# Gate and up both as seven products of half sums, their blocks interleaved

## The chip, the core and the metric

The kernel runs on one core of a Trainium2 chip. A core has five engines with a queue each: TensorE (PE in the profile; PEld is its weight loads), VectorE (DVE), ScalarE (ACT), GpSimd (POOL), and SyncE (SP), which only issues DMAs here. SBUF holds the operands; TensorE writes its products to PSUM, eight banks of 512 f32 columns for each of 128 partitions. The metric is device time in microseconds of one execution; lower is better.

## What is computed

A layer norm of x (2048 tokens x 512), a linear-attention branch A, a gated branch B, and their sum with x. The change lies in B's first two matrix products, gate and up:

```python
def _B_ref(x, w_gate, w_up, w_down):          # x: 2048 x 512
    g = jnp.einsum("bsd,df->bsf", x, w_gate)  # w_gate: 512 x 1792
    u = jnp.einsum("bsd,df->bsf", x, w_up)    # w_up:   512 x 1792
    h = g * u
    return jnp.einsum("bsf,fd->bsd", h, w_down)

x = A_x
xn = _layernorm(x, axis=-1)
return x + _A_ref(xn, A_wqkv, A_w_phi, A_wo) + _B_ref(xn, B_w_gate, B_w_up, B_w_down)
```

Branch A makes features from Q and K (exponentials of a projection, of both signs, each normalised), sums K's features times V over all tokens, and reads that sum out with Q's features.

## The kernel before

**Tiling.** The 512 model columns are four slices of 128 (contracted over), the 1792 gate and up columns are 14 slices `ft`, and tokens are 16 tiles of 128, or four groups `sg` of 512. The normalised tokens lie transposed in `xnT`. A product "weights slice x 512 tokens" is a group of four matmuls of 512 columns into one PSUM bank. `U(ft, sg)` makes gate and up in this plain way: the gate bank goes through a ScalarE copy (`ge`) to a bf16 slot, and VectorE multiplies the up bank by it (`h`) into `hT`.

**Seven products.** For token groups 1 and 2 and the pairs `(ft, ft+7)` with `ft` below `NB = 6`, `up` is made as a 2 x 2 block product (rows: `ft` and `ft+7`; columns: the two token groups; contraction split into two halves) with seven half products in place of eight (`BLOCK`, L821). A half product is two matmuls of 512 columns. It needs sums of token blocks, X1 to X4 (`XSUMS`, L781: eight VectorE steps, once), and sums of weight blocks, S1 to S4 (`WSUMS`, L792: four GpSimd steps of 256 columns for each block, two slots in `Su_v`). The steps of a block: P1 goes to bank `pa` and is copied by ScalarE to a second bank `c` (the seed); P2 is added on `c`; P6, P5 and P3 are added to `pa` one after the other, with what stands there read out in between (a snapshot by ScalarE, an add by VectorE); P7 and P4 go to bank `pb`. Gate is made plainly beside it (`G`, L800): four groups of four matmuls per block, spread between the block's products (L1072 to L1078).

**Down.** The product with `w_down` is of the same seven-product kind (`DOWN_STEPS`, pairs of token tiles), with sums T of `w_down` and S of `h` on GpSimd (L737 too, 512 and 896 columns wide). Its VectorE steps (L961) add the residual x.

**Banks.** In the block stage banks 0 and 1 are `pa` and `pb`, banks 6 and 7 gather K times V, and banks 2 to 5 are a ring from which `nb()` (L624) hands out one after the other: to gate products, K features, V, the seed bank.

**Order of work.** The program adds steps in one order (the loop at L1111: for each token tile K, V, then as many `units` as `PACE` asks). `_plan` (L199) then plays this list forward with a cost for each step and writes a fixed order for every queue: of the steps ready within a window of 60 ns it takes the one with the lowest `prio`, then the lowest place in the program. On the chip each queue runs in that order; a step waits on semaphores for what it needs. The costs: a matmul `n / 2.4 + 2.5` ns (L459), a VectorE step `60 + 1.045 n` (L452), a ScalarE step `50 + 0.835 n` (L444); `prio` is 0 everywhere.

**Lines in the profile.** L482 all matmuls; L437 ScalarE copies, exponentials and the seeds; L737 the sums (X on VectorE, the others on GpSimd); L679 reduces of K and Q features; L685 and L687 their even-up on GpSimd; L712 V's eviction on VectorE; L813 the gated product of a block; L819 its adds; L765 the gated product of `U`; L961 the down stage's adds.

Of the kernel before, what the change touches and what calls it, by code (L numbers as in the profile page):

```python
# [21 lines left out]
NQ = D // 128  # L22
# [327 lines left out]
NB = 6  # L350
NSW = 2
# [9 lines left out]
def _build(nc, es, A_x, A_wqkv, A_w_phi, A_wo, B_w_gate, B_w_up, B_w_down, out):  # L361
# [102 lines left out]
    def seed(o, src, name):  # L464
        act_op(o, src, name=name)
        seeded[(o.offset % 4096) // 512] = True
# [55 lines left out]
    def load_x(eng, t0, n, after=None):  # L522
        o = sbv("x", t0 * 512, n * 512)
        return sc.dma(eng, o.rearrange("p (t d) -> p t d", t=n),
               x_flat[t0 * 128:(t0 + n) * 128, :].rearrange("(t p) d -> p t d", p=128), n * 131072,
               writes=[o], name=f"x{t0}", after=after)
# [97 lines left out]
    def nb():  # L624
        b = ring_banks[0][rp[0] % len(ring_banks[0])]
        rp[0] += 1
        return b
# [44 lines left out]
    def features(Et, w, t, sm, name):  # L672
        b = nb()
        mm(group(bank(b), [(xnT(q, t * 128, 128), Wp_v[:, w, q, :]) for q in range(NQ)]), name=f"{name}{t}")
        ev = Et.rearrange("p (h s f) -> p h s f", h=H, s=2)
        src = bank(b).rearrange("p (h f) -> p h f", h=H)
        act_op(ev[:, :, 0, :], src, func=ACTF.Exp, name=f"{name}e{t}")
        act_op(ev[:, :, 1, :], src, func=ACTF.Exp, scale=-1.0, name=f"{name}e{t}")
        dve(lambda e: e.tensor_reduce(out=sm, in_=Et.rearrange("p (h f) -> p h f", f=16), axis=AX.X, op=ALU.add),  # L679
            [Et], [sm], cost=1130.0, name=f"{name}r{t}")  # L680
        return ev
# [87 lines left out]
    Su_v = sbv("tf", 0, NSW * 1024).bitcast(F16).rearrange("p (r w k j) -> p r w k j", r=NSW, w=4, k=2)  # L769
    sn_v = sbv("oring", 0, 3 * 512).bitcast(F16).rearrange("p (r s) -> p r s", r=3)  # L770
    snc = [0]
    gw = {}

    def snap():
        snc[0] += 1
        return sn_v[:, snc[0] % 3, :]
# [15 lines left out]
    def WSUMS(ft):  # L792
        S1, S2, S3, S4 = (Su_v[:, ft % NSW, w] for w in range(4))
        A = lambda i, k: wA(wu_v, i, k, ft)
        sums(POOL, S3, A(0, 0), A(1, 0), ALU.subtract, f"w3.{ft}")
        sums(POOL, S1, A(1, 0), A(1, 1), ALU.add, f"w1.{ft}")
        sums(POOL, S2, S1, A(0, 0), ALU.subtract, f"w2.{ft}")
        sums(POOL, S4, A(0, 1), S2, ALU.subtract, f"w4.{ft}")

    def G(ft, sg):  # L800
        i = gctr[0] % 6
        gctr[0] += 1
        g = sbv("gring", i * 512, 512) if i < 4 else sbv("tf", 2048 + (i - 4) * 512, 512)
        gw[ft, sg] = g
        b = nb()
        mm(group(bank(b), [(wg_v[:, q, ft * 128:(ft + 1) * 128], xnT(q, sg * 512, 512)) for q in range(NQ)]),
           name=f"g{ft}.{sg}")
        act_op(g, bank(b), name=f"ge{ft}.{sg}")

    def gated(ft, sg, src):  # L810
        h = hT_v[:, ft, hs(sg * 512):hs(sg * 512) + 512]
        g = gw[ft, sg]
        dve(lambda e: e.tensor_tensor(out=h, in0=src, in1=g, op=ALU.mult), [src, g], [h], name=f"h{ft}.{sg}")  # L813
# [4 lines left out]
    def add(o, src, sn, name):  # L818
        dve(lambda e: e.tensor_tensor(out=o, in0=src, in1=sn, op=ALU.add), [src, sn], [o], name=name)  # L819

    def BLOCK(ft, banks):  # L821
        ft2 = ft + NF // 2
        A = lambda i, k: wA(wu_v, i, k, ft)
        S1, S2, S3, S4 = (Su_v[:, ft % NSW, w] for w in range(4))
        X1, X2, X3, X4 = (Tx_v[:, w] for w in range(4))
        pa, pb = bank(banks[0]), bank(banks[1])
        st = {}

        def p1():
            xprod(pa, A(0, 0), xB(0, 1), True, f"b1.{ft}")  # L830
            st["c"] = bank(nb())
            seed(st["c"], pa, f"sd.{ft}")

        def p7():
            xprod(pb, S3, X3, True, f"b7.{ft}")
            st["p7"] = snap()
            act_op(st["p7"], pb, name=f"s7.{ft}")

        def p2():
            xprod(st["c"], A(0, 1), xB(1, 1), False, f"b2.{ft}")  # L840
            gated(ft, 1, st["c"])

        def p6():
            xprod(pa, S2, X2, False, f"b6.{ft}")
            st["u2"] = snap()
            act_op(st["u2"], pa, name=f"s2.{ft}")

        def p4():
            xprod(pb, A(1, 1), X4, False, f"b4.{ft}")
            add(pb, pb, st["u2"], f"a4.{ft}")  # L850
            gated(ft2, 1, pb)

        def p5():
            xprod(pa, S1, X1, False, f"b5.{ft}")
            add(pb, pa, st["p7"], f"a5.{ft}")
            gated(ft2, 2, pb)

        def p3():
            xprod(pa, S4, xB(1, 2), False, f"b3.{ft}")
            gated(ft, 2, pa)  # L860
# [208 lines left out]
    blocks = [BLOCK(ft, (0, 1)) for ft in range(NB)]  # L1069
    gs = [(G, f, sg) for ft in range(NB) for sg in (1, 2) for f in (ft, ft + NF // 2)]  # L1070
    units += [(XSUMS, XENG), (WSUMS, 0), (WSUMS, 1)] + gs[:4]
    for ft in range(NB):  # L1072
        p1, p7, p6, p2, p4, p5, p3 = blocks[ft]
        g4 = gs[4 * ft + 4:4 * ft + 8]
        seqs = [(p1,), (p7,)] + g4[:1] + [(p6,), (p2,)] + g4[1:2] + [(p4,)] + g4[2:3] + [(p5,)] + g4[3:] + [(p3,)]
        if ft + NSW < NB:
            seqs.append((WSUMS, ft + NSW))
        units += seqs  # L1078
# [53 lines left out]
    assert ui[0] >= NA  # L1132
    down = DOWN_STEPS(0)
# [91 lines left out]
```

## Time and profile before

| what | before |
|---|---|
| median of 4 runs | 217.71 us (215.18 to 218.83) |
| the profiled execution | 217.41 us, its span 215.4 us |
| granted TensorE clock | 1.000 |
| TensorE matmul busy | 208.1 us, 1609 recorded |
| VectorE, ScalarE, GpSimd busy | 153.6, 113.2, 138.1 us |
| HBM read, written | 8.67 MB, 2.10 MB |

The span runs from the first to the last instruction; the time of an execution has some 2 us more around it. Matmuls are pipelined: the duration of one, 379 ns for 512 columns, is its latency, and the next starts before it ends. A row of a group reads: line, engine, operation, output and inputs with their shapes, count, then busy us, mean ns of one, and the idle time before such instructions with what ended it.

### The profile page before, as it was taken

What the parts mean: (1) busy time and instruction counts of PE and PEld (TensorE: products, weight loads), DVE (VectorE), ACT (ScalarE), POOL (GpSimd) and SP (SyncE); (2) the same over time, 40 slices, a digit from 0 to 9 for tenths busy, and PEclk for the clock granted to TensorE, in tenths of its full rate; (3) what the DMA queues carried; (4) which work ended last, traced back from release to release, by engine and by line L of the source; (5) the groups of instructions that cost most, each with busy time, mean ns of one, the idle gap of its engine ahead of it and who ended that gap; (6) DMA issues with size and microseconds to landing.
All of it is one profiled execution on the core that took longest, in us unless ns stands there. A gap on an engine that the chain in (4) does not pass through costs nothing.

```text
span 215.4 us, 4228 instructions
## 1 busy us (share of the span) xinstructions
PE 208.1 (97%) x1619; PEld 138.6 (64%) x1642; DVE 153.6 (71%) x301; ACT 113.2 (53%) x286; POOL 138.1 (64%) x167
## 2 busy tenths in 40 slices
PE   8999999959999999999999999999999999999995
PEld 2775444425445444444546788898888888888984
DVE  4857599774948687695987884786666776568663
ACT  4656999769885759787732432334333243342000
POOL 4070644249999999995490289784977779422540
PEclk9999999999999999999999999999999999999999
DMA  5999799891100000222020145154173433514421
GB/s 171 325 258 358 208 138 87 249 264 24 27 0 0 3 0 0 49 50 52 0 49 3 36 80 131 24 77 97 27 124 71 99 75 71 127 30 96 96 77 52
DMA packets 48660, 19.96 MB, mean 93 GB/s; under 512 B 37376, under 2 KB 48640, under 8 KB 48640
## 3 DMA queue, kind: packets, MB, share of 16 engines
q1 hardware_dynamic: 47968, 19.36, 39.5%
q10 hardware_dynamic: 672, 0.33, 0.6%
q8 instruction: 13, 0.21, 0.4%
q14 instruction: 7, 0.06, 0.1%
HBM read 8.67 MB, written 2.10 MB: 50 GB/s over the span
## 4 chain that ended last, share of the span: by engine, by line
PE 82%; ACT 5%; DVE 5%; DMA 4%; issue 1%; POOL 1%; SPq 1%; DVEq 0%
PE ps L482 82%; ACT arena L437 5%; DMA arena<-in_B_w_up_dram 2%; DVE arena L679 2%; DVE arena L737 2%; DMA arena<-arena 1%; SPq L173 1%; DVE arena L712 1%; POOL arena L687 0%; POOL arena L605 0%; DVE arena L765 0%; POOL arena L685 0%; DVE arena L871 0%; DVE arena L961 0%; ACT arena L715 0%
## 5 line engine op out<-in xcount | busy, mean ns | idle before, releaser
L482 PE MATMUL ps<-arena 128*128 128x256 bf16 (+5 forms) x1609 | 203.8, 287 | 4.1 <-DVE arena L712 2.4
L482 PEld LDWEIGHTS ps<-arena 128*128 128x128 bf16 (+1 forms) x1632 | 137.3, 98 | 71.1 <-DVE arena L712 3.0
L437 ACT ACTIVATE arena<-ps 128x512 bf16<-128x512 f32 (+3 forms) x167 | 83.1, 534 | 72.6 <-PE ps L482 68.8
L737 POOL TENSOR_TENSOR arena<-arena 128x896 f16<-128x896 f16 (+3 forms) x72 | 91.9, 1288 | 24.3 <-PE ps L482 18.8
L679 DVE TENSOR_REDUCE arena<-arena 128x64 f32<-128x1024 bf16 x32 | 38.8, 1215 | 14.1 <-ACT arena L437 14.1
L437 ACT ACTIVATE arena<-arena 128x32 f32<-128x32 f32 (+4 forms) x96 | 28.9, 313 | 12.6 <-DVE arena L679 9.7
L687 POOL TENSOR_TENSOR arena<-arena 128x512 bf16<-128x512 bf16 x32 | 33.8, 1057 | 1.2
L961 DVE TENSOR_TENSOR arena<-ps,arena 128x256 f32<-128x256 f32 (+1 forms) x56 | 23.5, 421 | 11.7 <-PE ps L482 11.5
L685 POOL TENSOR_TENSOR arena<-arena 128x32 f32<-128x32 f32 x32 | 8.5, 266 | 24.6 <-ACT arena L437 24.6
L813 DVE TENSOR_TENSOR arena<-ps,arena 128x512 f16<-128x512 f32 x24 | 16.3, 687 | 7.5 <-PE ps L482 7.2
L871 DVE TENSOR_TENSOR arena<-ps,arena 128x256 f16<-128x256 f32 x32 | 13.4, 420 | 10.6 <-ACT arena L437 10.6
L712 DVE TENSOR_TENSOR arena<-ps,arena 128x512 bf16<-128x512 f32 x16 | 10.9, 683 | 2.0 <-PE ps L482 1.4
L765 DVE TENSOR_TENSOR arena<-ps,arena 128x512 f16<-128x512 f32 x14 | 9.6, 684 | 3.7 <-PE ps L482 2.3
L596 DVE BATCH_NORM_STATS2 arena<-arena 128x6 f32<-128x512 bf16 x16 | 10.5, 675 | 2.3 <-DMA arena<-in_A_x_dram 2.1
L919 DVE TENSOR_TENSOR arena<-ps,arena 128x512 bf16<-128x512 f32 x16 | 11.0, 690 | 0.4
L819 DVE TENSOR_TENSOR ps<-ps,arena 128x512 f32<-128x512 f32 x12 | 8.3, 694 | 3.4 <-PE ps L482 3.2
L605 POOL TENSOR_SCALAR arena<-arena 128x1 f32<-128x1 f32 x12 | 3.0, 265 | 9.6 <-ACT arena L437 9.6
L578 POOL TENSOR_TENSOR arena<-arena 128x128 bf16<-128x128 bf16 x4 | 1.6, 426 | 8.7 <-DMA arena<-in_A_w_phi_dram 8.7
L915 DVE RECIPROCAL arena<-arena 128x32 f32<-128x32 f32 x16 | 5.6, 350 | 0.4
L1038 PE MATMUL ps<-const-bfloat16-1.0 128*128 128x512 bf16 x10 | 4.4, 626 | 0.8 <-PEq L1210 0.8
L737 DVE TENSOR_TENSOR arena<-arena 128x512 f16<-128x512 bf16 x8 | 3.9, 531 | 1.1 <-DMA arena<-arena 1.1
L715 ACT ACTIVATE arena<-arena 128x32 bf16<-128x32 f32 x16 | 3.7, 231 | 0.3
(20 smaller groups left out, 24.0 us busy)
## 6 DMA issues: line engine op xcount, KB each, us to landing
arena<-in_B_w_down_dram SPq DMA_DIRECT2D x1, 1792.0 KB, 7.9
out_dram<-arena SPq DMA_DIRECT2D x14, 128.0 KB, 2.0
arena<-in_A_x_dram SPq DMA_DIRECT2D x3, 512.0 KB, 8.9
arena<-in_B_w_gate_dram SPq DMA_DIRECT2D x1, 768.0 KB, 7.4
arena<-in_B_w_up_dram SPq DMA_DIRECT2D x1, 768.0 KB, 7.9
arena<-arena SPq DMA_TRANSPOSE x44, 3.0
arena<-in_B_w_gate_dram SPq DMA_DIRECT2D x2, 256.0 KB, 4.7
arena<-in_B_w_gate_dram SPq DMA_DIRECT2D x1, 512.0 KB, 6.2
```

Source lines behind the costliest of these rows:

```text
L437: return e.activation(out=out_ap, in_=in_ap, func=func, scale=scale, **kw)
L482: ins = e.matmul(o, lhsT=l, rhs=r, start=s, stop=p, skip_group_check=True)
L596: dve(lambda e, t=t: e.bn_stats(stats_v[:, t, :], x_tile(t)), [x_tile(t)], [stats_v[:, t, :]], cost=560.0, name=f"st{t}", win=win)
L679: dve(lambda e: e.tensor_reduce(out=sm, in_=Et.rearrange("p (h f) -> p h f", f=16), axis=AX.X, op=ALU.add), [Et], [sm], cost=1130.0, name= ...
L687: pool(lambda e: e.tensor_tensor(out=ev[:, :, 1, :], in0=ev[:, :, 1, :], in1=ratio[:, :, None].to_broadcast([128, H, 16]), op=ALU.mult), [ ...
L712: dve(lambda e: e.tensor_tensor(out=o1, in0=src, in1=rp_[:, :, :, None].to_broadcast([128, 8, 4, 16]), op=ALU.mult), [src, rs_v[:, t % 4, ...
L737: fn = lambda e: e.tensor_tensor(out=out_, in0=a_, in1=b_, op=op)
L765: dve(lambda e: e.tensor_tensor(out=h, in0=bank(bu), in1=g, op=ALU.mult), [bank(bu), g], [h], name=f"h{ft}.{sg}")
L813: dve(lambda e: e.tensor_tensor(out=h, in0=src, in1=g, op=ALU.mult), [src, g], [h], name=f"h{ft}.{sg}")
L871: dve(lambda e: e.tensor_tensor(out=h, in0=bank(b, 256, 256), in1=g, op=ALU.mult), [bank(b, 256, 256), g], [h], name=f"h{ft}.{s_lo}")
L919: dve(lambda e: e.tensor_tensor(out=ov, in0=src, in1=wv4[:, :, :, None].to_broadcast([128, 8, 4, 16]), op=ALU.mult), [src, w], [o], cost=6 ...
L961: dve(lambda e: e.tensor_tensor(out=out_, in0=in_ps, in1=in_sb, op=ALU.add), [in_ps, in_sb], [out_], cost=328.0, name=f"{name}.{p}")
```

## The change

Gate is also made of seven half products for the six pairs. `BLOCK` takes a kind, `"u"` or `"g"`: gate blocks use bank 1 as `pa`, up blocks bank 0. `pb` is no fixed bank any more: P7 takes one from the ring and holds it until after P4, and the seed bank is held from P1 until after P2; `nb()` passes over held banks. P5's sum of an up block takes another ring bank. Where an up block ends in gated products, a gate block writes its results to gate slots: two by ScalarE copies, two straight from VectorE's adds.

A gate block stands one block ahead of its up block, and the products of up block `ft` and gate block `ft+1` are interleaved. GpSimd makes weight sums for both kinds. The gate sums, gate snapshots and a seventh gate slot lie in the space of x tiles 4 to 11, which have been normalised by then; two DMAs load these tiles again before the down stage. Seeds, snapshots and gate copies get priority -1 on ScalarE, adds and gated products -1 on VectorE. The reduce of the features can be cut into `RS` parts; `RS` is 1, so it is as before.

```diff
+RS = 1
+PA = -1
+PD = -1
@@
-    def nb():
-        b = ring_banks[0][rp[0] % len(ring_banks[0])]
-        rp[0] += 1
+    held = set()
+
+    def nb(hold=False):
+        assert not held.issuperset(ring_banks[0])
+        while True:
+            b = ring_banks[0][rp[0] % len(ring_banks[0])]
+            rp[0] += 1
+            if b not in held:
+                break
+        if hold:
+            held.add(b)
         return b
@@
-    Su_v = sbv("tf", 0, NSW * 1024).bitcast(F16).rearrange("p (r w k j) -> p r w k j", r=NSW, w=4, k=2)
-    sn_v = sbv("oring", 0, 3 * 512).bitcast(F16).rearrange("p (r s) -> p r s", r=3)
-    snc = [0]
+    xz = layout["x"] + 4 * 512
+    S_w = {"u": sbv("tf", 0, NSW * 1024), "g": arena[:, xz:xz + NSW * 1024]}
...
+    sn_v = {"u": sbv("oring", 0, 3 * 512), "g": arena[:, xz + 2048:xz + 2048 + 3 * 512]}
...
+    gslots = ([sbv("gring", i * 512, 512) for i in range(4)] + [sbv("tf", 2048 + i * 512, 512) for i in range(2)]
+              + [arena[:, xz + 3584:xz + 4096]])
@@
-    def BLOCK(ft, banks):
+    def BLOCK(kind, ft, ba):
...
         def p1():
-            xprod(pa, A(0, 0), xB(0, 1), True, f"b1.{ft}")
-            st["c"] = bank(nb())
-            seed(st["c"], pa, f"sd.{ft}")
+            xprod(pa, A(0, 0), xB(0, 1), True, "b1" + nm)
+            st["ci"] = nb(True)
+            st["c"] = bank(st["ci"])
+            seed(st["c"], pa, "sd" + nm)
 
         def p7():
-            xprod(pb, S3, X3, True, f"b7.{ft}")
-            st["p7"] = snap()
-            act_op(st["p7"], pb, name=f"s7.{ft}")
+            st["bi"] = nb(True)
+            st["b"] = bank(st["bi"])
+            xprod(st["b"], S3, X3, True, "b7" + nm)
+            st["p7"] = snap(kind)
+            act_op(st["p7"], st["b"], name="s7" + nm, prio=PA)
...
         def p4():
-            xprod(pb, A(1, 1), X4, False, f"b4.{ft}")
-            add(pb, pb, st["u2"], f"a4.{ft}")
-            gated(ft2, 1, pb)
+            pb = st["b"]
+            xprod(pb, A(1, 1), X4, False, "b4" + nm)
+            if kind == "u":
+                add(pb, pb, st["u2"], "a4" + nm)
+                gated(ft2, 1, pb)
+            else:
+                add(gslot(ft2, 1), pb, st["u2"], "a4" + nm)
+            held.discard(st["bi"])
 
         def p5():
-            xprod(pa, S1, X1, False, f"b5.{ft}")
-            add(pb, pa, st["p7"], f"a5.{ft}")
-            gated(ft2, 2, pb)
+            xprod(pa, S1, X1, False, "b5" + nm)
+            if kind == "u":
+                pt = bank(nb())
+                add(pt, pa, st["p7"], "a5" + nm)
+                gated(ft2, 2, pt)
+            else:
+                add(gslot(ft2, 2), pa, st["p7"], "a5" + nm)
@@
-    units += [(XSUMS, XENG), (WSUMS, 0), (WSUMS, 1)] + gs[:4]
+    gb = [BLOCK("g", ft, 1) for ft in range(NB)]
+    ub = [BLOCK("u", ft, 0) for ft in range(NB)]
+    units += [(XSUMS, XENG), (WSUMS, "g", 0), (WSUMS, "u", 0), (WSUMS, "g", 1), (WSUMS, "u", 1)]
+    p1, p7, p6, p2, p4, p5, p3 = gb[0]
+    units += [(f,) for f in (p1, p7, p2, p6, p4, p5, p3)]
     for ft in range(NB):
...
         if ft + NSW < NB:
-            seqs.append((WSUMS, ft + NSW))
-        units += seqs
+            units.append((WSUMS, "g", ft + NSW))
+        u = ub[ft]
+        g = gb[ft + 1] if ft + 1 < NB else [None] * 7
+        p1, p7, p6, p2, p4, p5, p3 = u
+        q1, q7, q6, q2, q4, q5, q3 = g
+        units += [(f,) for f in (p1, p7, p2, p6, q1, q7, p4, q2, p5, q6, p3, q4, q5, q3) if f is not None]
+        if ft + NSW < NB:
+            units.append((WSUMS, "u", ft + NSW))
@@
     assert ui[0] >= NA
+    load_x(SP, 4, 4, name="rx")
+    load_x(SP, 8, 4, name="rx")
```

## The prediction, made before the changed kernel was run

> **What bounds the kernel now.** I read the page's forty slices first, then a table by stretches of time, then the timeline around the one hole, then the groups by shape for prices. The slices (each digit is the busy share of 5.4 us, in tenths):
>
> ```profile
> PE   8999999959999999999999999999999999999995
> DVE  4857599774948687695987884786666776568663
> ACT  4656999769885759787732432334333243342000
> POOL 4070644249999999995490289784977779422540
> ```
>
> TensorE is full from start to end except for one slice, the ninth (43 to 48 us). GpSimd is full through the ten slices after it. The table by stretches gives busy us of each engine; the block stage (the 512-token products of gate and up for tokens 512 to 1535) runs from about 41 to 116 us:
>
> ```profile
> 41.00:47.00 6.00, 3.62 (x23) 1.62 (x22) 6.00 (x12) 3.97 (x12) 2.11 (x4) 1.00 1.13 323
> 47.00:58.00 11.00, 10.92 (x69) 5.54 (x71) 6.46 (x10) 9.85 (x23) 11.00 (x14) 1.00 0.20 48
> 82.00:94.00 12.00, 11.95 (x70) 5.69 (x70) 8.65 (x12) 9.73 (x26) 12.00 (x17) 1.00 0.12 23
> 105.00:116.00 11.00, 10.89 (x75) 5.78 (x76) 9.43 (x14) 4.98 (x14) 6.26 (x6) 1.00 0.13 24
> ```
>
> Columns: stretch, TensorE, weight loads, VectorE, ScalarE, GpSimd, then clock, DMA share, GB/s. Before 47 us VectorE is busy without a break and TensorE waits; from 47 us TensorE is busy without a break at the full clock (1.00), beside ScalarE at 9.85 of 11 early and VectorE at 9.43 of 11 late. The hole in TensorE's timeline, and VectorE's work in it:
>
> ```profile
> 39.72 4.95 PE L482 MATMUL ps<-arena 128*128 128x512 bf16 x28
> 47.02 3.19 PE L482 MATMUL ps<-arena 128*128 128x512 bf16 x14 [2.36 <-DVE arena L712]
> ```
> ```profile
> 39.21 0.43 DVE L737 TENSOR_TENSOR arena<-arena 128x512 f16<-128x512 bf16 x1 [1.09 <-DMA arena<-arena]
> ...
> 41.88 2.35 DVE L737 TENSOR_TENSOR arena<-arena 128x512 f16<-128x512 bf16 x4
> 44.16 1.21 DVE L679 TENSOR_REDUCE arena<-arena 128x64 f32<-128x1024 bf16 x1
> 45.29 1.08 DVE L737 TENSOR_TENSOR arena<-arena 128x512 f16<-128x512 bf16 x3
> 46.29 0.68 DVE L712 TENSOR_TENSOR arena<-ps,arena 128x512 bf16<-128x512 f32 x1
> ```
>
> The token sums X (L737 on VectorE, eight of them) stand ahead of the V eviction (L712), and that eviction holds the PSUM bank that the next gate product needs. Prices by shape (busy us, mean ns):
>
> ```profile
> L482 PE MATMUL ps<-arena 128*128 128x512 bf16 x413 | 98.3, 379 | 3.6 <-DVE arena L712 2.4
> L437 ACT ACTIVATE arena<-ps 128x512 bf16<-128x512 f32 x110 | 60.4, 597 | 31.6 <-PE ps L482 28.6 <-DVE arena L813 2.6
> L737 POOL TENSOR_TENSOR arena<-arena 128x256 f16<-128x256 bf16 x22 | 14.5, 667 | 0.6 <-DMA arena<-in_B_w_up_dram 0.4
> L482 PE MATMUL ps<-arena 128*128 128x512 f16 x48 | 14.1, 379 | 0.0
> L437 ACT ACTIVATE arena<-ps 128x512 f16<-128x512 f32 x12 | 7.1, 594 | 0.8 <-PE ps L482 0.8
> L819 DVE TENSOR_TENSOR ps<-ps,arena 128x512 f32<-128x512 f32 x12 | 8.3, 694 | 3.4 <-PE ps L482 3.2
> ```
>
> The 379 ns is latency. The price of a 512-column matmul is its spacing: 14 of them take 3.19 us, so (3.19 - 0.379) / 13 = 0.216 us; f16 operands show the same 379.
>
> **TensorE.** Per block, four gate products of four matmuls (16) become seven of two (14). Six blocks: 12 matmuls fewer, 12 x 0.216 = 2.6 us, all on the path, since TensorE is what ends every stretch from 47 us on. A rule speaks against counting this: the Trainium skill, "Perfetto Trace Analysis", section Identifying the Most-Contended Engine, says that matmul busy time is no measure of headroom and weight-load busy time (or FLOPs against peak) is. Weight loads fill 5.54 of 11 us here, half; taken by that figure TensorE would have room and the 12 matmuls would be worth 0. The spacing of 0.216 us for 512 columns leaves no room between matmuls (one load of 98 ns hides behind each), so I take 2.6.
>
> **Start of the stage.** X still waits for the transposes that land at 39.2 us and still takes until 46.4. Before, TensorE had three plain gate products (2.6 us), which need no X, ahead of the hole. After, the first gate block can run P1 and P2 without X; P7 needs X3 (there at 43.9), P6 needs X2 (45.7), P4 needs X4 (46.4). Five products of 0.43 = 2.16 us get done by the time V's bank comes free at 47.0, against 2.6 before: the hole costs 0.4 more. Bounds: 2.4 us gained if the queue's order fills it, 2 us lost if P7 and what stands behind it on TensorE (a KV product, K of tile 5) come late and push their own followers.
>
> **GpSimd.** Four more weight sums per block, 24 x 0.667 = 16.0 us. The first two gate sets (5.3 us) read weights and scratch that are free once tiles 4 to 7 are normalised (about 27 us), and GpSimd idles some 6 us between there and 39 us, so they lie beside other work. The other 10.7 us fall into the saturated stretch, and what yields is the W_down sums (L737, 512 wide: 12 x 1.154) and the first pairs' S sums, which now run early as filling. GpSimd idles 3.3, 0.8, 0.9, 5.3 and 4.5 us at gaps between 99 and 124 us, 14.8 in all, which takes 10.7: cost 0, up to 2 us if W_down sums or the first S3 come after P7 of the down stage wants them (it starts at 117). A second rule: the Trainium skill, "SBUF — State Buffer", section Who interferes with whom, says a VectorE instruction with two SBUF inputs blocks against a GpSimd one that reads SBUF. The trace has it: four X sums took 2.35 us while K's even-up multiply (L687, 42.50 for 1.12 us) ran on GpSimd, where three took 1.08. By the rule at its worst each of the eight X sums could wait out one gate weight sum, 8 x 0.667 = 5.3 us more hole. I take 0, since the first sets fit in before 39 us, and the new VectorE adds have one input in PSUM.
>
> **VectorE.** Two more adds per block, 12 x 0.69 = 8.3 us, one block earlier than the gated products that use them. VectorE goes from about 8.7 to 10 of 12 us in the middle stretch: covered, but at 85%. **ScalarE.** 24 gate evictions (14.3 us) become 30 seeds, snapshots and evictions (6 x 5 x 0.597 = 17.9): 3.6 more, covered, tight in 47 to 58, where it has 1.15 us free.
>
> **Queue order and banks.** The order of each queue is frozen by the planner, which counts 595 ns for a 512-wide VectorE step and 478 for a ScalarE one; the rows say 690 and 597. So every hand-over is some 0.1 us late where TensorE has nothing in reserve. Today the four plain gate products per block are that reserve; after, both kinds are chains of hand-overs. Three to four tight hand-overs in each of five double blocks at 0 to 0.1: 0 to 2 us, I take 0.8, near the low end because the page shows only 4.1 us of waits for all 1609 matmuls. The priorities for chain steps cost nothing of themselves; what they delay is K's and Q's exponentials and reduces and V's evictions, which hold ring banks. Bounds -0.5 to +5, taken as 0 here; it is the slow rival.
>
> **Reload of x.** Two DMAs of 512 KB on SP, 0.5 us of issue each. They wait for the last gate blocks' reads (near 100 to 110 us); behind them stand the fourth Q transpose (107) and the first output transposes (120). Tile 4's x is first read in the down stage's third pair, near 144 us; x loads took 8.9 us to land in the crowded start and the DMA share here is 0.1 to 0.3. Cost 0; if the wait held SP to 120, the 1 MB would cost at most 1 to 2 us.
>
> **Sum.** -2.6 + 0.4 + 0.8 = -1.4 us on the profiled execution, whose time is 217.4 (span 215.4 and 2.0 around it): 216.0. The median of the runs is 0.3 higher: 216.3.
>
> **Rivals.** (1) Likeliest, 216.3, own range 214.8 to 219: 0.42. (2) The hole closes: products of up's first block, which need only tokens and a free bank, are drawn forward into it. Then 2.6 + 2.4 to 2.85 are saved: 212.5. For it: P1 and P2 of both kinds need no X. Against: VectorE is busy for all six us of that stretch, and everything else waits for it. 0.20. (3) Slower: the ring runs out of banks. The ring has four banks in this stage (2 to 5). In a double block up's P7 bank, gate's P2 bank and gate's P7 bank are all held between gate's P7 and up's P4, leaving one for K and V, whose evictions (two exponentials of 0.6, or 0.68 on VectorE) now stand behind the chain steps. If two such products per double block wait one eviction and one chain step, 0.6 + 0.6, half of them with a 0.43 filler ahead, TensorE loses about 1.8 us per double block, 9 in five: 217.7 - 2.2 + 9 = 224.5. It decides beyond a 2% loss from 1.3 us per double block (6.6 in all). For it: the only hole today is just this, a bank held by a late eviction, and ScalarE, VectorE and GpSimd stand at 80 to 100%. Against: from 47 us on nothing of the kind shows. 0.33. (4) The change doesn't shorten the end: late W_down or S sums on GpSimd give the 2.2 us back at 114 to 120: 217.7 to 218.5. 0.05.
>
> **Numbers.** Faster by over 2% (below 213.4) is rival 2 alone: 0.20. Slower by over 2% (above 222.1) is rival 3: 0.33. Within 2%, about what a measurement of this kernel can tell from no change: 0.47. The predicted time is the likeliest, 216.3. Both signs together hold more than it does, so the 8-in-10 range runs from the middle of rival 2 to just past rival 3's value, 212.5 to 225.0.
>
> **What would show it.** Right: TensorE has 12 fewer 512-wide matmuls, its hole before the first blocks lasts 2.5 to 3.5 us, waits after 47 us stay under 2 us, and the down stage's first product starts near 114.5 us instead of 116.1. Rival 2: no hole over 1 us. Rival 3: repeated TensorE waits of 0.5 to 2 us between 50 and 110 us, released by ScalarE exponentials or VectorE L712. Rival 4: a wait on GpSimd L737 at 113 to 120 us. A longer hole at 41 to 47 beside weight sums on GpSimd would make my reading of the port rule wrong; a stall of x reads near 144 us that of the reload.

## The result, and the profile after

| | before | after |
|---|---|---|
| median of the runs | 216.65 us (64 runs) | 215.35 us (43 runs) |
| range | 215.14 to 218.83 | 214.53 to 217.20 |
| profiled execution, its span | 217.41, 215.4 us | 214.46, 212.5 us |

The ratio is 0.9963, with an interval of 0.9947 to 0.9978: faster, by less than 2%. The kernel before, at 217.71 over its first four runs, stands at 216.65 over 64.

The times after are not one cluster. Of 44 executions 27 have a granted clock of 0.999 or more (median 214.99) and 17 have 0.991 or 0.992 (median 216.68). Of 80 executions of the kernel before beside the experiments below, one had less than the full clock. The profiled execution after is one at the full clock. The page's forty slices after:

```profile
PE   8899999699999999999999999999999999999995
DVE  4847599996969698999977866686666876568653
ACT  4656989679986889888722533424433243332000
POOL 4070697439999999999999695875958779422640
PEclk9999999999999999999999999999999999999999
```

TensorE's one thin slice is still there, one place earlier (37 to 43 us). GpSimd is now full over thirteen slices in a row, where it was over nine. The table by stretches of the kernel after (stretch, length, TensorE, weight loads, VectorE, ScalarE, GpSimd, clock, DMA share, GB/s):

```profile
41.00:47.00 6.00, 4.38 (x27) 2.12 (x29) 5.93 (x11) 4.49 (x12) 2.33 (x5) 1.00 0.99 274
47.00:58.00 11.00, 10.95 (x77) 5.58 (x77) 9.04 (x14) 10.71 (x28) 11.00 (x17) 1.00 0.07 15
82.00:94.00 12.00, 11.95 (x69) 5.61 (x69) 11.12 (x16) 10.62 (x29) 12.00 (x18) 1.00 0.23 44
105.00:116.00 11.00, 10.76 (x77) 5.84 (x78) 8.46 (x15) 2.61 (x6) 11.00 (x8) 1.00 0.33 84
```

ScalarE rose from 9.85 to 10.71 of 11 us in the second row and VectorE from 8.65 to 11.12 of 12 in the third, and TensorE beside them has as little idle time as before. The last row has lost a little: 10.76 instead of 10.89, with GpSimd full. Line numbers have moved: L485 are the matmuls, L440 ScalarE's copies, exponentials and seeds, L753 the sums, L838 the adds of a block, L694 K's and Q's reduces, L701 and L703 their even-up, L728 V's eviction, L781 the gated product of `U`. The groups by shape (busy us, mean ns, idle before them):

```profile
L485 PE MATMUL ps<-arena 128*128 128x512 bf16 x353 | 85.1, 379 | 1.2
L485 PE MATMUL ps<-arena 128*128 128x512 f16 x96 | 26.3, 379 | 2.0 <-DVE arena L753 2.0
L753 POOL TENSOR_TENSOR arena<-arena 128x256 f16<-128x256 bf16 x40 | 26.4, 676 | 1.5 <-PE ps L485 1.0 <-DMA arena<-in_B_w_up_dram 0.3
L838 DVE TENSOR_TENSOR ps<-ps,arena 128x512 f32<-128x512 f32 x12 | 8.3, 692 | 2.1 <-PE ps L485 1.5 <-ACT arena L440 0.7
L838 DVE TENSOR_TENSOR arena<-ps,arena 128x512 bf16<-128x512 f32 x12 | 8.0, 682 | 0.0
L440 ACT ACTIVATE ps<-ps 128x512 f32<-128x512 f32 x12 | 7.1, 594 | 2.3 <-PE ps L485 2.0
```

The 512-column matmuls are 449 instead of 461: 12 fewer (f16 ones have doubled, bf16 ones gone down by 60). VectorE's adds and ScalarE's seeds have doubled. The 2.0 us before the f16 matmuls is the hole, and what ends it is now an X sum (L753). TensorE's timeline around it (start, busy, and idle before it with what ended it):

```profile
36.74 3.87 PE L485 MATMUL ps<-arena 128*128 128x512 bf16 x24
42.57 5.18 PE L485 MATMUL ps<-arena 128*128 128x512 f16 x29 [1.95 <-DVE arena L753]
```

and VectorE's timeline in the same stretch:

```profile
37.76 1.29 DVE L753 TENSOR_TENSOR arena<-arena 128x512 f16<-128x512 bf16 x3 [0.51 <-DMA arena<-arena]
38.98 1.20 DVE L694 TENSOR_REDUCE arena<-arena 128x64 f32<-128x1024 bf16 x1
40.10 0.67 DVE L781 TENSOR_TENSOR arena<-ps,arena 128x512 f16<-128x512 f32 x1
40.70 0.67 DVE L728 TENSOR_TENSOR arena<-ps,arena 128x512 bf16<-128x512 f32 x1
41.30 2.22 DVE L753 TENSOR_TENSOR arena<-arena 128x512 f16<-128x512 bf16 x4
```

The first group of matmuls ends with V's product of tile 3. Next in TensorE's queue is P7 of the first gate block, ahead of P1 and P2, and it needs X3. X3 comes in the last line, behind K's reduce (L694), a gated product of U (L781) and a V eviction (L728), 2.5 us of VectorE work, none of which needs X. The first of its four sums is the second half of X3. It took 1.21 us, and each of the other three 0.41; GpSimd's even-up of K ran beside it:

```profile
41.30 1.21 DVE L753 TENSOR_TENSOR arena<-arena 128x512 f16<-128x512 bf16 x1
```
```profile
41.17 1.06 POOL L703 TENSOR_TENSOR arena<-arena 128x512 bf16<-128x512 bf16 x1
```

So 0.8 us of the hole is this meeting. All five traces with this order have it (1.21 to 1.23 us for that sum), and the kernel before had the like (1.27 us for the same sum, in the 2.35 us of the prediction's row).

**Where the time went.** A single span says little to within 1 us: over the traces of this study V's product of tile 3, ahead of the hole, starts anywhere between 39.6 and 41.2 us. So TensorE's time was cut at fixed matmuls, start to start, and each part split into work (512 columns at 0.216 us, others by the planner's n / 2.4 + 2.5 ns; matmuls without a record are counted from the kernel's own order) and the rest, called lost:

| us | before | after |
|---|---|---|
| hole (V's product of tile 3 to that of tile 4), lost | 2.54 | 2.13 |
| from there to the last K times V product, lost | 0.14 | 0.52 |
| from there to the last matmul, lost | 0.12 | 0.13 |
| all three: work | 170.00 | 167.41 |
| all three: lost | 2.80 | 2.79 |

Work is down by 2.59 us; what is lost is the same. It lies mostly in two places: the hole, and one wait near 109 us that costs TensorE 0.3. The wait in TensorE's table of waits, as its weight loads show it (sum, count, longest) and, below it, GpSimd's timeline there:

```profile
PEld ps L485 <- POOL arena L703: 0.6, 1, 0.6
```
```profile
104.60 1.89 POOL L753 TENSOR_TENSOR arena<-arena 128x896 f16<-128x896 f16 x1
...
106.66 1.89 POOL L753 TENSOR_TENSOR arena<-arena 128x896 f16<-128x896 f16 x1
108.49 1.06 POOL L703 TENSOR_TENSOR arena<-arena 128x512 bf16<-128x512 bf16 x1
```

The even-up of the last K (L703) stands behind sums of 1.89 us on a GpSimd that has no pause; the last K times V product needs it and stands at the head of TensorE's queue.

### The profile page after: what moved, and what is told of

It is laid out like the page before. It is cut to its first block, busy times and chain, and to the rows that moved or that the text cites. A ratio compares the mean times of both kernels' runs of the same rounds, so it can differ in the third digit from the quotient of the medians.

```text
span 212.5 us, 4265 instructions
## 1 busy us (share of the span) xinstructions
PE 205.1 (97%) x1607; PEld 136.8 (64%) x1630; DVE 160.0 (75%) x313; ACT 115.5 (54%) x292; POOL 152.7 (72%) x191
## 3 DMA queue, kind: packets, MB, share of 16 engines
q1 hardware_dynamic: 49024, 20.41, 40.8%
## 4 chain that ended last, share of the span: by engine, by line
PE 71%; POOL 17%; issue 3%; DMA 2%; DVE 2%; ACT 2%; SPq 1%; DVEq 0%
PE ps L485 71%; POOL arena L753 12%; POOL arena L703 3%; DMA arena<-in_B_w_up_dram 2%; ACT arena L440 1%; POOL arena L701 1%; SPq L173 1%; DVE arena L753 1%; DVE arena L694 1%; DVE arena L728 0%; DVE arena L781 0%; ACT ps L440 0%; DVE arena L910 0%; DVE arena L1000 0%; DVEq L343 0%
## 5 line engine op out<-in xcount | busy, mean ns | idle before, releaser
L485 PE MATMUL ps<-arena 128*128 128x256 bf16 (+5 forms) x1597 | 201.2, 286 | 4.1 <-DVE arena L753 2.0
L485 PEld LDWEIGHTS ps<-arena 128*128 128x128 bf16 (+1 forms) x1620 | 135.6, 98 | 70.1 <-DVE arena L753 2.4
L753 POOL TENSOR_TENSOR arena<-arena 128x256 f16<-128x256 bf16 (+3 forms) x96 | 107.7, 1139 | 21.9 <-PE ps L485 16.4
L440 ACT ACTIVATE arena<-ps 128x512 bf16<-128x512 f32 (+3 forms) x167 | 82.9, 537 | 67.4 <-PE ps L485 63.4
L694 DVE TENSOR_REDUCE arena<-arena 128x64 f32<-128x1024 bf16 x32 | 38.9, 1215 | 11.2 <-ACT arena L440 11.2
L440 ACT ACTIVATE arena<-arena 128x64 f32<-128x64 f32 (+4 forms) x96 | 29.0, 319 | 10.5 <-DVE arena L694 8.3
L703 POOL TENSOR_TENSOR arena<-arena 128x512 bf16<-128x512 bf16 x32 | 33.8, 1059 | 0.7
L701 POOL TENSOR_TENSOR arena<-arena 128x32 f32<-128x32 f32 x32 | 8.4, 263 | 13.2 <-ACT arena L440 13.2
L728 DVE TENSOR_TENSOR arena<-ps,arena 128x512 bf16<-128x512 f32 x16 | 10.9, 683 | 4.8 <-PE ps L485 4.3
L781 DVE TENSOR_TENSOR arena<-ps,arena 128x512 f16<-128x512 f32 x14 | 9.5, 682 | 4.2 <-PE ps L485 3.4
L958 DVE TENSOR_TENSOR arena<-ps,arena 128x512 bf16<-128x512 f32 x16 | 11.0, 689 | 0.4
L838 DVE TENSOR_TENSOR ps<-ps,arena 128x512 f32<-128x512 f32 x12 | 8.3, 692 | 2.1 <-PE ps L485 1.5
L440 ACT ACTIVATE ps<-ps 128x512 f32<-128x512 f32 x12 | 7.1, 594 | 2.3 <-PE ps L485 2.0
L838 DVE TENSOR_TENSOR arena<-ps,arena 128x512 bf16<-128x512 f32 x12 | 8.0, 682 | 0.0
L1077 PE MATMUL ps<-const-bfloat16-1.0 128*128 128x512 bf16 x10 | 3.9, 562 | 0.8 <-PEq L1256 0.8
```

What stands on the lines that cost most here:

```text
L440: return e.activation(out=out_ap, in_=in_ap, func=func, scale=scale, **kw)
L485: ins = e.matmul(o, lhsT=l, rhs=r, start=s, stop=p, skip_group_check=True)
L694: dve(lambda e, ei=ei, so=so: e.tensor_reduce(out=so, in_=ei.rearrange("p (h f) -> p h f", f=16), axis=AX.X, op=ALU.add), [ei], [so], cost ...
L701: pool(lambda e: e.tensor_tensor(out=ratio, in0=smv[:, :, 0], in1=rc, op=ALU.mult), [sm, rc], [ratio], 180.0, name=f"{name}q{t}")
L703: pool(lambda e: e.tensor_tensor(out=ev[:, :, 1, :], in0=ev[:, :, 1, :], in1=ratio[:, :, None].to_broadcast([128, H, 16]), op=ALU.mult), [ ...
L728: dve(lambda e: e.tensor_tensor(out=o1, in0=src, in1=rp_[:, :, :, None].to_broadcast([128, 8, 4, 16]), op=ALU.mult), [src, rs_v[:, t % 4, ...
```

## The experiments

Two theories stood at the start. The first, that of the hole: what is lost is lost before the first gate block, because VectorE's order puts X late, and the hole also makes the granted clock fall in some executions. Its rival, that of the saturated engines: from 47 us on the engines beside TensorE are the bound (GpSimd first, then the hand-overs of the longer chains), and the hole is of little weight. All ratios are against the kernel before on the same chip. The experiments were spread over three chips, so runs on different chips are compared by ratio.

**The changed kernel again.** No edit.

> The changed kernel itself, on the chip of these comparisons. If some of its runs show a granted clock of 0.992 here too, the clock loss belongs to the kernel; if all are at 1.00, it belongs to the chip, and the median is 214.7 to 215.2 (0.992 to 0.994 of the kernel before).

Measured: 214.97 us, ratio 0.9966 [0.9938, 0.9993], as the first time. Eight of 12 executions at the full clock (median 214.85), four at 0.992 (216.66). Its trace lost 3.26 us in the hole against 2.13, with the same order on every queue: the X sums start at 39.17 us instead of 37.76, as the DMA that they wait for lands later, and P7 starts at 43.80. So the hole differs from execution to execution by about 1 us.

**X first (the changed kernel).**

```diff
-            dve(fn, parts(a_) + parts(b_), parts(out_), cost=60.0 + 0.53 * n, name=name)
+            dve(fn, parts(a_) + parts(b_), parts(out_), cost=60.0 + 0.53 * n, prio=-2, name=name)
```

> The changed kernel with the eight X sums first on VectorE (priority -2); TensorE's planned order is the same as in the changed kernel. Theory A, TensorE and its hole bound the time: the hole of 2.44 us before the first gate block (waiting for X3) shrinks to under 1 us, the span falls by 1.5 to 2.4 us against the changed kernel's 212.5, and runs with a granted clock of 0.992 become rare because TensorE no longer idles that long; median 213.0 to 213.8. Theory B, GpSimd now bounds the block stage up to the last K even-up (109.6 us, which TensorE waits for): closing the hole moves the wait to that place, and at most 0.6 us is gained: span 212 or more.

Measured: 214.39 us, 0.9898 [0.9873, 0.9924], all five runs at the full clock. P7 now follows V's product without a wait. An idle time of 1.12 us is left behind it, and another releaser ends it:

```profile
36.69 5.85 PE L485 MATMUL ps<-arena 128*128 128x512 bf16 x39
43.66 4.01 PE L485 MATMUL ps<-arena 128*128 128x512 bf16 x17 [1.12 <-DVE arena L781]
```

The next product there is K's of tile 5. It needs the bank that the gated product of U (L781) reads, and that step now stands behind the X sums and K's reduce. The hole's loss is 1.45 us. That gave the next edit.

**X first, and the gated product that frees that bank ahead of the rest.** As above, and in `U`:

```diff
-            name=f"h{ft}.{sg}")
+            name=f"h{ft}.{sg}", prio=-3 if (ft, sg) == (13, 0) else 0)
```

> As the X-first version, and the gated product of gate slice 13 (which frees the bank that the first gate block's P1 needs) is put ahead of K's reduce too. Theory A: the remaining holes of 1.6 and 0.5 us go, and the time falls by another 1 to 1.6 us against X-first: span 211.1 to 211.7, median 213.0. Theory B (GpSimd bounds the stage): the TensorE wait for K's last even-up near 109 us grows by as much, median stays at 214.0 to 214.4.

Measured: 214.07 us, 0.9896 [0.9870, 0.9921], all five runs at the full clock: the lowest median of the study, by ratio level with X first. TensorE and VectorE in its timeline:

```profile
36.79 6.28 PE L485 MATMUL ps<-arena 128*128 128x512 bf16 x42
43.79 3.88 PE L485 MATMUL ps<-arena 128*128 128x512 bf16 x16 [0.71 <-ACT ps L440]
```
```profile
38.20 1.69 DVE L753 TENSOR_TENSOR arena<-arena 128x512 f16<-128x512 bf16 x4 [0.44 <-DMA arena<-arena]
39.81 0.68 DVE L781 TENSOR_TENSOR arena<-ps,arena 128x512 f16<-128x512 f32 x1
40.41 1.41 DVE L753 TENSOR_TENSOR arena<-arena 128x512 f16<-128x512 bf16 x4
```

All eight sums are done at 41.8, and the idle time is 0.71 us, ended by ScalarE's seed (L440), which P2 needs. The hole's loss is 1.14 us. Both times missed what the theory of the hole had named (213.0 to 213.8, then 213.0) and lie where its rival had put them. The rival's reason is not in the traces: the loss from the hole to the last K times V product is 0.58 and 0.68 us here, against 0.52 to 0.62 with the hole untouched, so hardly any of the gain came back as a wait there. Against the mean of five traces with the hole untouched (2.47 us) the two edits took 1.0 and 1.3 us off it; at the full clock they gave some 0.5 and 0.8, and the rest was not traced to a place.

**The kernel before, X late.** The mirror image: there the X sums stood ahead of the V eviction for which TensorE waited.

```diff
-            dve(fn, parts(a_) + parts(b_), parts(out_), cost=60.0 + 0.53 * n, name=name)
+            dve(fn, parts(a_) + parts(b_), parts(out_), cost=60.0 + 0.53 * n, prio=1, name=name)
```

> The kernel before with the X sums behind other VectorE work (priority +1), so that the V eviction comes before the last X sums. Theory A: its hole of 2.85 us, which waits for that eviction, shrinks to about 1 us and the time falls by 1.5 to 2 us, to about 214.8 (0.991): as much as the whole change brought. Rival: VectorE is full there and the hole only moves to the first product that needs X: 216.3 to 216.7.

Measured: 215.63 us, 0.9964 [0.9941, 0.9986]: by ratio, this one word is worth to the kernel before as much as the whole change. It gave 0.9 us where 1.5 to 2 had been expected. Its hole lost 0.75 us instead of 2.54; in TensorE's timeline nothing over 0.25 is left:

```profile
36.63 6.89 PE L482 MATMUL ps<-arena 128*128 128x512 bf16 x37
43.77 2.59 PE L482 MATMUL ps<-arena 128*128 128x512 bf16 x18 [0.25 <-DVE arena L712]
46.51 1.25 PE L482 MATMUL ps<-arena 128*128 128x512 bf16 x5 [0.16 <-ACT arena L437]
```

**The hole filled with matmuls that nothing reads.** Eight products of 512 columns in the changed kernel, ten in the kernel before, put at the hole in TensorE's queue. They are meant to fill TensorE's idle time and leave all waits in place. The core of both edits (FILL adds n such matmuls; the chain fixes their place):

```diff
+    sc.chain("v3 fill0 fill1 fill2 fill3 fill4 fill5 fill6 fill7 b7g.0")
```
```diff
+    sc.chain("k5 fill0 fill1 fill2 fill3 fill4 fill5 fill6 fill7 fill8 fill9 g7.2")
```

> The changed kernel with eight dummy matmuls of 512 columns (1.7 us, results unused, no other order changed) on TensorE in its hole. Theory A: the hole itself costs what it did, span at full clock 212.5 to 213.3, but the granted clock is 1.00 in all runs and the upper group of run times near 216.7 us is gone: median 214.6 to 215.1. Rival: the clock loss has nothing to do with the hole: about 4 in 10 runs stay at 0.992.

> The kernel before with ten dummy matmuls (2.2 us, results unused) in its own hole of 2.85 us. Theory A: if the hole costs the kernel before clock as well, its runs at a clock under 1 go and its median falls by up to 0.5 us, to about 216.2; the two kernels then stand 1.5 to 2 us apart at full clock (the 2.6 us of matmuls less 0.4 at the hole and the hand-overs). Rival: the hole has no part in the clock: nothing moves, 216.6.

Measured, changed kernel: 215.53, 0.9959 [0.9937, 0.9980], all 12 at the full clock, from 215.11 to 216.14. No execution has a lower clock, but the time is not better, a miss (214.6 to 215.1 had been expected): the fill-in products did not fit entirely in the hole. In TensorE's timeline they start late, behind a V eviction, and P7 follows:

```profile
42.20 1.92 PE L1083 MATMUL ps<-const-bfloat16-1.0 128*128 128x512 bf16 x8 [0.83 <-DVE arena L728]
43.96 3.87 PE L485 MATMUL ps<-arena 128*128 128x512 f16 x23
```

In the kernel after, P7 starts 1.27 us after the four X sums begin (41.30, 42.57). Here they begin at 42.06, so X3 is there near 43.3, and P7 starts at 43.96: by this estimate the fill-in products cost 0.6 us. Measured, kernel before: 217.25, 1.0041 [1.0026, 1.0057], slower, which was a miss. There was no fall of the clock to win back, and ten products are 2.2 us of work for which an execution with a shorter hole would have to wait. No trace shows that: the one kept is of the fastest of the twelve, and it has a hole of 2.19 us with 2.16 of matmuls in it.

**A longer hole.** Two reduces of no use (1.2 us each) on VectorE, ahead of X:

```diff
+    sc.chain("vs2 late0 late1 Xs1.1")
```

> The changed kernel with two dummy reduces (2.3 us, results unused) on VectorE ahead of the last sum that the first gate block's P7 needs, so that TensorE's hole lasts some 4 to 5 us. Theory A, the clock is lost to the hole: nearly all runs show a granted clock of 0.992 or less, in the trace a stretch of a lower clock near 43 to 48 us, and the median rises by the 2 us of the longer hole and 1.7 us of clock more, to 218 or over. Rival, the clock has another cause: 3 to 4 in 10 runs at 0.992 as in the changed kernel, median 216.5 to 217.3.

Measured: 217.64, 1.0036 [1.0004, 1.0067]. Three executions at the full clock (median 216.47) and eight below it (217.79): more falls than the 3 to 4 in 10 of the rival, but not nearly all, and a median below the 218 expected. The profiled one is of the second kind, and its table by stretches shows the fall (columns as above; the clock is the number after GpSimd's):

```profile
40.00:44.00 4.00, 1.26 (x13) 0.66 (x11) 4.00 (x6) 1.72 (x5) 1.32 (x2) 1.00 1.03 346
44.00:48.00 4.00, 2.83 (x7) 1.10 (x9) 4.00 (x8) 1.34 (x3) 0.67 (x1) 0.59 0.98 217
48.00:52.00 4.00, 4.00 (x20) 1.80 (x19) 2.53 (x4) 3.47 (x10) 2.67 (x3) 0.98 0.00 2
```

The trace's clock record has one step down to half and one up again, 3.413 us apart, from 44.71 to 48.12 us; matmuls in between start 0.43 us apart instead of 0.216. The rows agree: at half clock for a time t, the mean falls by t/8 in a stretch of 4 us, so (0.41 + 0.02) x 8 = 3.4 us of half clock, which is 1.7 us of matmul time lost. That is the distance of the two groups of the changed kernel's times (216.68 - 214.99 = 1.69).

The Trainium skill, "TensorE: Matmul & The Clock Gate", section What's actually happening, has a free-running activity window of that length, and the fall after one idle window. This trace agrees: TensorE stood still from 41.26 to 44.95 us, 3.69 us, and the 3.413 us ahead of the step down lie just inside. For the changed kernel the rule looks too strict: the idle times in its traces are 1.95 to 3.08 us, shorter than a window. No fall is among these traces, but the lower group less 1.7 us stands at 214.98, where the others are, so its holes can hardly have been longer.

All executions, by what was done to the hole:

| kernels | lost in the hole (trace) | at 0.992 or less |
|---|---|---|
| changed, hole untouched (first result, again, no T sums, no reload, no priorities) | 2.13 to 3.26 | 17 of 44, 4 of 12, 3 of 12, 4 of 12, 0 of 6 |
| changed, longer hole | 5.42 | 8 of 11 |
| changed, hole smaller (X first, X and gated product first, NB of 7) | 1.12 to 1.45 | 0 of 16 |
| changed, hole filled | 2.76, with 1.7 of it matmuls | 0 of 12 |
| changed, X3 first (below) | 2.04 | 0 of 12 |
| before, hole untouched | 2.54 | 1 of 80 |
| before, X late or filled | 0.75, 2.19 (2.16 of it matmuls) | 0 of 24 |

X first and the filled kernel ran on a chip on which the changed kernel itself was not run, so for these 17 executions the chip is not ruled out as the reason. The other 11 with a smaller hole, and the 12 with X3 first, stand on chips where kernels with the hole untouched did fall (7 of 30, and 4 of 12).

**No priorities.** `PA = 0`, `PD = 0`.

> The changed kernel with the chain-step priorities set to 0. Prediction's value: 0 (within 0.3 us of the changed kernel). If the priorities carry the change: 1 us or more slower, with new TensorE waits on ScalarE or VectorE between 50 and 105 us.

Measured: 214.94, 0.9934 [0.9912, 0.9956], all six at the full clock; the changed kernel at the full clock had 214.85 beside it. The priorities are worth nothing either way. None of six at a lower clock is no evidence: at one in three it comes up in 9 of 100 such draws.

**No sums of w_down on GpSimd.** `TSUMS` is left out (its output set once to zero), 16.5 us less for GpSimd; the down stage then lacks them.

> The changed kernel without the sixteen GpSimd steps that sum w_down (16.5 us of GpSimd work; T1, T2, T4 are zero and T3 is w_down itself, so the down products are not the reference's). Theory A: GpSimd is full but not the bound: only the wait of 0.63 us before the last K times V goes: span 211.9 to 212.5, median within 0.6 us of the changed kernel. Theory B: GpSimd bounds the stage: 2 us or more faster.

Measured: 214.88, 0.9945 [0.9916, 0.9974]; at the full clock 214.71 against 214.85. GpSimd's timeline near the last even-up (L706 in this kernel):

```profile
105.28 0.27 POOL L704 TENSOR_TENSOR arena<-arena 128x32 f32<-128x32 f32 x1 [2.45 <-ACT arena L440]
105.62 1.06 POOL L706 TENSOR_TENSOR arena<-arena 128x512 bf16<-128x512 bf16 x1
```

GpSimd now waits 2.45 us for its input, the even-up runs at 105.62 instead of 108.49, and the loss between hole and last K times V product falls from 0.52 to 0.22. So the whole fullness of GpSimd costs 0.3 us on TensorE at that one place, and the rival theory falls in its first part.

**No reload of x.** The two DMAs are left out, and the down stage adds what lies in those tiles' space.

> The changed kernel without the two DMAs that load x tiles 4 to 11 again (those tiles' residual is scratch, so the output differs there). Prediction's value: the reload costs 0, so the same time as the changed kernel, 214.7 to 215.4. If it held SyncE's queue or the DMA engines: 0.5 to 2 us faster.

Measured: 215.42, 0.9959 [0.9931, 0.9987]; at the full clock 215.09. The time from V's product of tile 3 to the last matmul is 170.30 us against 170.20 with the reload: it costs nothing.

**X3 first, with K's reduce ahead of the rest.** An order of VectorE's queue by hand:

```diff
+    sc.chain("Xs1.0 Xs1.1 kr3 h13.0 Xs0.0 Xs0.1 Xs2.0 Xs2.1 vs2 Xs3.0 Xs3.1 vs3 kr4")
```

> The changed kernel with VectorE's order in the hole written out: the sum X3 that P7 needs, K's reduce, the gated product that frees P1's bank, then the other sums, and the V eviction before the next reduce. Theory A: TensorE's loss between the V products of tiles 3 and 4 (2.1 us in the changed kernel, 1.35 in the version with X and slice 13 first) falls under 1 us, no run at a clock of 0.992, median 213.3 to 213.8. Theory B, what is gained there is lost at the wait for GpSimd's last even-up: 214.0 or more.

Measured: 215.51, 0.9946 [0.9926, 0.9967], a miss; the hole lost 2.04 us. TensorE, ScalarE and VectorE in its timeline tell why:

```profile
44.19 2.11 PE L485 MATMUL ps<-arena 128*128 128x512 bf16 x9 [1.29 <-ACT arena L440]
46.76 0.99 PE L485 MATMUL ps<-arena 128*128 128x512 f16 x3 [0.47 <-DVE arena L753]
```
```profile
42.13 0.55 ACT L440 ACTIVATE arena<-arena 128x64 f32<-128x64 f32 x2 [1.62 <-DVE arena L694]
42.70 0.23 ACT L731 ACTIVATE arena<-arena 128x32 bf16<-128x32 f32 x1
42.84 1.55 ACT L440 ACTIVATE arena<-ps 128x512 bf16<-128x512 f32 x3
```
```profile
42.61 2.83 DVE L753 TENSOR_TENSOR arena<-arena 128x512 f16<-128x512 bf16 x4
45.36 0.68 DVE L728 TENSOR_TENSOR arena<-ps,arena 128x512 bf16<-128x512 f32 x1
45.96 0.75 DVE L753 TENSOR_TENSOR arena<-arena 128x512 f16<-128x512 bf16 x2
```

P7 runs without a wait. The larger loss, 1.2 us, is before P1 (the first of its two matmuls has no record, so the row shows 1.29). Its bank holds K's product of tile 4 until ScalarE's two exponentials have read it (first two of the three at 42.84), and these stand behind steps of K's tile 3, for which ScalarE waits 1.62 us until K's reduce is done. In the two kernels with X first the planner had put these exponentials ahead of those steps. A smaller one, in the second row, is before P4. It needs X4, the two sums of the last row, and the four X sums ahead of them took 2.83 us where in the kernel with the lowest median four took 1.41 and 1.69: GpSimd's even-up (43.23, for 1.11 us) and a weight sum (44.31, for 0.85) ran beside them. That is the port rule of the prediction at work; the 1.2 us before P1 would be there without it.

**All seven pairs in half products.** `NB = 7`, on the kernel with X and that gated product first.

> The version with X and slice 13 first, and all seven pairs of slices as half sums (NB = 7): four matmuls fewer for each of gate and up's last pair, 0.86 us. GpSimd gets eight more weight sums (5.3 us), VectorE four adds. Theory A, TensorE's work still sets the time: 0.5 to 0.9 us faster than that version, 213.2 to 213.6. Theory B, GpSimd or VectorE is at its limit: no gain or slower, 214.0 to 216, with TensorE waits on GpSimd L756 or VectorE near 100 to 120 us.

Measured: 215.36, 0.9932 [0.9906, 0.9958], no gain on the kernel that it is built on (0.9896, on another chip; the intervals overlap). In the traces TensorE's work is 0.86 us less (166.55), its loss 4.08 us instead of 1.95. Of the 2.13 more, 1.02 lie between the hole and the last K times V product. The two largest terms in its table of waits (sum, count, longest):

```profile
PEld ps L485 <- ACT arena L440: 3.9, 11, 0.7
PEld ps L485 <- ACT ps L440: 3.5, 8, 1.2
```

These overlap with weight loads that would have been early anyway, so they add up to more than is lost; but they are waits on ScalarE's seeds and snapshots, of the kind that the rival theory expected at six pairs. They come with the seventh, in which no plain product of this stage is left as reserve; that this is the reason is argued, since the seventh pair also adds weight sums and adds. Another 1.14 us are a single wait far behind the block stage, at a product of the down stage that needs a DMA's transpose:

```profile
199.44 2.73 PE L485 MATMUL ps<-arena 128*128 128x256 f16 x27 [0.97 <-DMA arena<-arena]
```

Whether other executions have it, one trace can't tell.

## Why the prediction was right, and where it was not

The forecast was 216.3 against 217.71, a ratio of 0.9935; measured were 215.35 against 216.65, 0.9963. The case was the likeliest one, within 2% and a little faster. That 1.4 us less had been forecast and 1.3 were measured is in part luck: the hand-overs and the start of the stage were charged too much, and the fall of the clock was not charged at all. Step by step:

- **TensorE, -2.6.** Right: 170.00 - 167.41 = 2.59 us of work, and the time from V's product of tile 3 to the last matmul fell by as much. The rule on weight-load time, by which it would have been 0, doesn't hold here: in a stage of 512-column matmuls without gaps the loads are busy half of the time and there is still no room.
- **Start of the stage, +0.4.** The working was wrong and the sum near. P1 and P2 do not run ahead of the hole: P7 stands first in the queue, and the bank of P1 comes free only when ScalarE has read K's product of tile 4, at 42.0 us in the trace after. In exchange the hole ends with X3, at 42.5, instead of with V's bank. At the full clock the step is worth about nothing: five traces with this order (first result, again, no priorities, no T sums, no reload) lost 2.13, 3.26, 2.33, 2.39 and 2.23 us, mean 2.47, against 2.54. But this is the step that failed in what it left out. An idle TensorE was priced by its length alone. In 28 of 86 executions of the kernels with this hole untouched the mean clock was 0.992 or less, which is the price of one fall of 3.4 us, 1.7 us each. In the first result's runs that is 17/44 x 1.69 = 0.65 us in the mean, and it moves the median from 214.99 to 215.35. At the full clock the change is worth 216.65 - 214.99 = 1.66 us, where 1.4 had been forecast.
- **GpSimd, 0 up to 2.** It cost 0.3, at another place: not at P7 of the down stage but at the last K's even-up. The kernel without T sums shows it.
- **Hand-overs, +0.8.** Too large. The loss between hole and last K times V product rose by 0.52 - 0.14 = 0.38 us, and 0.3 of it is the even-up. The hand-overs themselves cost 0.1. The kernel with seven pairs lost 1.0 us more in that stretch, which is nearer to what the forecast feared.
- **VectorE, ScalarE, priorities, reload: 0.** Right in the cost: the two stretches above, the kernel without priorities and the one without the reload. VectorE was busy for 11.12 of 12 us in the middle stretch, though, where 10 had been forecast.
- **The port rule, 0.** Right as a difference, since both kernels pay it, and right that no gate weight sum met an X sum. But K's even-up did, at the very sum for which P7 waits: 1.21 us instead of 0.41, so 0.8 us of the hole could have been avoided. Where an order keeps the two apart (X first), no sum behind the first takes over 0.42 us.
- **Rival 2 (the hole closes).** It did not close of itself. P1 could have filled 0.4 us near its end, when its bank was free, and P2 waits for P1's seed; K's product of tile 5 (0.86 us), which stands behind them in the queue, had its bank from 40.8 us on, and that order was not tried. The two reorderings show that most of it was to be had: 0.9898 and 0.9896. The forecast's reason against it, that VectorE is busy throughout, was not the whole of it: the order of that work mattered, by 0.8 us at the full clock (214.85 - 214.07).
- **Rival 3 (banks run out).** Not seen: between 48 and 112 us no wait of TensorE's weight loads exceeds some 0.4 us but the one at the even-up. **Rival 4** came in at 0.3.
- **The signs.** The 12 matmuls fewer and waits under 2 us after 47 us came as named. The hole's idle time was 1.95 us, and 3.08 in the second trace, where 2.5 to 3.5 had been named. The down stage's first product starts at 110.7 us instead of 114.5, because the planner moved it ahead of plain products; as a sign of the time it was of no use.

The terms at the full clock, with the four traces of the changed queues that keep T sums for the middle part (0.52, 0.61, 0.62, 0.52, mean 0.57): -2.59 - 0.07 + (0.57 - 0.14) + (0.13 - 0.12) = -2.2, where the medians differ by 1.66. The remaining 0.5 was not traced to a place. It lies within the 1 us by which the start differs between traces, and the only trace of the kernel before as it stands is of an execution 0.76 us above its median.

**What stays open.** Why the clock almost never falls in the kernel before, whose hole has 2.36 us of idle time in its one trace, and falls in a third of the executions of the changed one, isn't settled. A longer hole made it more frequent, and with a smaller or filled hole it was not seen; but the kernel with X3 first kept 2.04 us of loss and full clock in 12 of 12. There the idle time is cut in pieces (1.29 and 0.47 us); whether the length of one stretch without matmuls is what counts was not tried. No execution of the changed kernel itself was profiled while the clock fell.

## What to carry over

A change that trades TensorE work for chains on other engines can pay nearly all the matmuls saved: with six pairs of seven the chains cost TensorE 0.1 us and a late even-up 0.3. The seventh pair saved 0.86 us and lost 1.0 in the same stage. When such a change brings a new operand (X3) to the head of TensorE's queue, the order of the engine that makes it has to be moved with it: in the kernel before, one priority was worth as much as the change. Such a new order moves the other queues too, so the wait to look for next can be on an engine that was not touched: with X3 first it was ScalarE. An idle time of 2 to 3 us on TensorE is to be judged by the granted clock of all executions as well as by its length.

## What was not expected of the hardware

The fall of the clock lasts 3.413 us where it was traced and costs 1.7 us, in 17 of 44 executions of one and the same kernel and in one of 80 of another with a hole of like size. V's product of tile 3 starts up to 1.6 us later in one trace than in another (39.6 to 41.2), and the hole of one kernel by 1.1 us (2.13 and 3.26 lost), so that parts of a span have to be compared from matmul to matmul, and over several traces.
